# Moving constants, a residual addition and FFN work between engines in a fused linear-attention and bilinear-FFN block

## The chip, the core and the metric

The kernel runs on one core of a Trainium2 chip. Its engines work in parallel, each through its own list of instructions in order, and wait for one another by semaphores: TensorE (PE in the profile) multiplies matrices into PSUM, VectorE (DVE), ScalarE (ACT) and GpSimd (POOL) work element by element, and SyncE (SP) issues the DMA transfers. PSUM has 8 banks of 128 x 512 float32; SBUF holds everything else. The metric is the device time of one execution in microseconds (us), lower is better.

## What is computed

x is 2048 x 512; all data are float32. c and w_mod give six vectors of 512: shifts sa and sb, scales ca and cb, gates ga and gb.

```python
x = A_x
mod = (_silu(c) @ w_mod).reshape(c.shape[0], 6, 1, -1)
sa, ca, ga, sb, cb, gb = (mod[:, 0], mod[:, 1], mod[:, 2], mod[:, 3], mod[:, 4], mod[:, 5])
h = _layernorm(x, axis=-1) * (1 + ca) + sa
x = x + ga * _A_ref(h, A_wqkv, A_wo)
h = _layernorm(x, axis=-1) * (1 + cb) + sb
x = x + gb * _B_ref(h, B_w_gate, B_w_up, B_w_down)
```

`_A_ref` is linear attention with 32 heads of 16: with phi(t) = (t + 1 where t > 0, else exp(t)) + 1e-6 it forms, for each head, kv = phi(k)^T v and z = the sum of phi(k) over all tokens, then o = phi(q) kv / (phi(q) z + 1e-6), and multiplies by wo. `_B_ref` is (h w_gate) * (h w_up), times w_down, with 1376 hidden features.

## The kernel before

**Tiling.** The 2048 tokens are 4 chunks of 4 token tiles of 128. A float32 operand of a product is split into a high part (rounded to the matmul's format by a copy on ACT, L167) and a low part (the rest, a subtraction on DVE or POOL, L168), and each product is three matmuls: high by high, high by low, low by high. `bank()` gives one of four working PSUM banks and `acc_bank()` one of four accumulation banks. All large SBUF tiles share 99 slots; a tile waits until the slot that it takes is free. The order of the instructions on each engine is the order of the program text: the schedule is written out by hand.

**The token loop (L361 to L404).** v is never formed: the loop sums phi(k)^T times the normalized x over all 16 token tiles in the four accumulation banks (`t_tile`). Step i projects the keys of tile i + 2 (`proj`, 12 matmuls), in some steps also queries, prepares phi (`phi_a`: three ACT operations, Relu, Exp and the addition of 1e-6; `phi_b`: one on DVE) and multiplies tile i. In step j = 1 of a chunk the next chunk is transposed and modulated (`Norm.transpose`, `Norm.modulated`): for each of four column blocks ACT applies scale and shift (L240), DVE casts the high part (L241) and subtracts (L242). `extra` hangs other work on single steps: splits of wq and wv, and the loads and sums of the remaining modulation vectors (`mod_start`).

**Between loop and FFN (L405 to L498).** wo is loaded and split, the sums are turned into the four 512 x 128 products `wp` that carry kv, wo and ga, and `den_p`, `den_r`, `den_b`, `den_c` divide phi(q) by its denominator: a product with z (on POOL for most tiles), a sum over each head, a reciprocal, and a multiplication in place.

**Attention output (`y_step`).** For token tile i, `turn` transposes phi(q) and splits it, `y_a` multiplies it by `wp` into an accumulation bank, and `y_b` adds x to the bank on DVE (L532), writes x and takes the row statistics for the second norm.

**FFN.** The 1376 hidden features are 11 tiles of 128 (the last 96). The first eight are worked off in pairs over two chunks at once, with seven block products in place of eight (`block`, L848; the loop at L978 has 8 steps of two blocks). The last three, `lone`, are worked off chunk by chunk in `ffn` (L592): for each f the gate and up products (24 matmuls into two banks), their product on DVE, its split, and the down product of the f before. `Left` prepares sums of four column blocks for the pair stage; for the second pair of chunks its steps are in the list `trickle`, from which `some(n)` takes n at given points. At those points (`s1`, `s2`, `s3`, `down`, `s4` of a block) there are also the split of the next weights (`right_split`: four ACT copies, four POOL subtractions), their loads and their sums.

## Time and profile before

| what | us |
|---|---|
| median of 3 runs | 595.63 (595.63 to 596.22) |
| the profiled execution | 595.54 |
| its span, first to last instruction | 593.8 |
| outside the span | 1.7 |
| TensorE, first matmul | 12.0 after the start |
| DVE, ACT, POOL busy | 400.6, 283.8, 207.1 |

Busy time of an engine is the union of its instructions' bars. Matmuls are pipelined: a bar of 0.39 us can begin 0.23 us after the one before, so bars overlap. Below, "idle" for PE is the time that no bar covers, and a wait is put down to the instruction whose end released it. A chain of waits is followed back from the last instruction of the program.

### The profile page before, as it was taken

Reading aid. Unit: us, or ns where it says so; the run is one execution under the profiler, and the core shown is the slowest. Engines: PE = TensorE matmul, PEld = TensorE weight load, DVE = VectorE, ACT = ScalarE, POOL = GpSimd, SP = SyncE. Lnnn points to the kernel's source line nnn. Section 1 sums busy time; section 2 is a strip of 40 time slices with the busy share of each in tenths; the row PEclk is TensorE's granted clock in tenths of the full one; section 3 lists DMA queues with packets and bytes.
Section 4 is the critical chain, followed back from the end, with each engine's and each line's share of the span. In section 5 each row is a group of like instructions: output and inputs, shape, how many; then the busy total and the mean of one; then the engine's idle time right before and its main releaser. Section 6 shows DMA issues by size and latency. Waiting matters only on the chain.

```text
span 593.8 us, 7258 instructions
## 1 busy us (share of the span) xinstructions
PE 563.6 (95%) x2548; PEld 456.1 (77%) x2548; DVE 400.6 (67%) x621; ACT 283.8 (48%) x489; POOL 207.1 (35%) x186
## 2 busy tenths in 40 slices
PE   1999998999899998999999999999999999999997
PEld 1777886788788876887877788878778888888885
DVE  6877396964879799865757548778785454545475
ACT  3497684747562821533152445453553444444430
POOL 1323012220412380000000108676684848383710
PEclk9999999999989999999999999999999999999999
DMA  8900122220500100002603215532259736120003
GB/s 287 349 2 1 54 88 72 71 72 0 148 1 0 72 1 1 36 36 86 198 36 107 71 38 141 177 130 84 97 189 357 279 106 213 35 72 0 2 2 141
DMA packets 46501, 57.17 MB, mean 96 GB/s; under 512 B 5152, under 2 KB 23584, under 8 KB 46464
## 3 DMA queue, kind: packets, MB, share of 16 engines
q1 hardware_dynamic: 46464, 56.71, 29.2%
q8 instruction: 20, 0.33, 0.2%
q14 instruction: 17, 0.14, 0.1%
HBM read 40.96 MB, written 15.73 MB: 95 GB/s over the span
## 4 chain that ended last, share of the span: by engine, by line
PE 74%; DVE 14%; ACT 8%; issue 2%; DMA 1%; POOL 0%; SPq 0%; DVEq 0%; ACTq 0%; POOLq 0%
PE bank L816 25%; PE acc L832 5%; PE acc L834 5%; PE acc L833 5%; PE bank L180 3%; PE bank L181 3%; PE bank L182 3%; PE bank L613 3%; PE bank L614 3%; PE bank L612 3%; PE acc L182 2%; PE acc L180 2%; PE acc L181 2%; DVE w L168 2%; PE acc L295 1%
## 5 line engine op out<-in xcount | busy, mean ns | idle before, releaser
L816 PE MATMUL bank<-h,w 128*128 128x512 f32 x672 | 156.4, 390 | 3.3 <-ACT kh L167 1.3
L816 PEld LDWEIGHTS bank<-h,w 128*128 128x128 f32 x672 | 125.8, 188 | 31.2 <-ACT bank L822 2.8
L168 POOL TENSOR_TENSOR w<-raw,w 128x512 fp32r<-128x512 f32 x26 | 37.3, 1454 | 75.6 <-ACT w L167 57.6
L167 ACT ACTIVATE kh<-phi 128x512 fp32r<-128x512 f32 (+1 forms) x60 | 37.2, 628 | 55.2 <-DVE phi L621 34.3
L802 POOL TENSOR_TENSOR w<-raw,w 128x256 fp32r<-128x256 f32 (+1 forms) x28 | 30.8, 1101 | 81.2 <-ACT w L795 81.2
L588 DVE TENSOR_TENSOR x<-acc,x 128x512 f32<-128x512 f32 x80 | 50.7, 680 | 4.1 <-PE acc L834 3.5
L168 DVE TENSOR_TENSOR kl<-phi,kh 128x512 fp32r<-128x512 f32 (+1 forms) x60 | 47.1, 794 | 9.4 <-ACT kh L167 8.7
L822 ACT ACTIVATE bank<-bank 128x512 f32<-128x512 f32 x32 | 18.6, 582 | 67.5 <-PE bank L816 67.5
L834 PE MATMUL acc<-w,kl 128*128 128x512 f32 x128 | 49.9, 390 | 0.0
L832 PE MATMUL acc<-w,kh 128*128 128x512 f32 x128 | 49.8, 389 | 0.0
L833 PE MATMUL acc<-w,kh 128*128 128x512 f32 x128 | 49.8, 389 | 0.0
L180 PE MATMUL bank<-w,h 128*128 128x512 f32 x120 | 48.7, 406 | 0.0
L181 PE MATMUL bank<-w,h 128*128 128x512 f32 x120 | 47.3, 394 | 1.0 <-DVE w L168 1.0
L182 PE MATMUL bank<-w,h 128*128 128x512 f32 x120 | 47.5, 396 | 0.0
L281 POOL TENSOR_TENSOR z<-z,phi 128x512 f32<-128x512 f32 x15 | 21.3, 1421 | 72.0 <-DVE phi L267 68.0
L217 POOL TENSOR_TENSOR rstd<-ve,half 128x4 f32<-128x4 f32 x8 | 9.8, 1231 | 96.3 <-DVE ve L216 96.3
L802 POOL TENSOR_TENSOR w<-t,w 128x512 fp32r<-128x512 f32 x28 | 39.3, 1405 | 0.0
L613 PE MATMUL bank<-h,w 128*128 128x512 f32 (+1 forms) x96 | 37.7, 392 | 0.3 <-DVE h L242 0.2
L612 PE MATMUL bank<-h,w 128*128 128x512 f32 (+1 forms) x96 | 37.8, 393 | 0.0
L614 PE MATMUL bank<-h,w 128*128 128x512 f32 (+1 forms) x96 | 37.5, 391 | 0.0
L225 ACT ACTIVATE n<-x,nmr,rstd 128x512 f32<-128x512 f32 x32 | 23.7, 803 | 20.9 <-DVE nmr L220 20.9
L903 DVE TENSOR_TENSOR g<-bank,u 128x512 f32<-128x512 f32 x16 | 11.0, 687 | 33.6 <-PE bank L816 33.6
(144 smaller groups left out, 1224.7 us busy)
## 6 DMA issues: line engine op xcount, KB each, us to landing
raw<-in_w_mod_dram SPq DMA_DIRECT2D x24, 256.0 KB, 3.8
raw<-in_B_w_down_dram SPq DMA_DIRECT2D x18, 256.0 KB, 3.0
x<-in_A_x_dram SPq DMA_DIRECT2D x16, 256.0 KB, 5.4
kept<-f SPq DMA_DIRECT2D x16, 256.0 KB, 2.0
f<-kept SPq DMA_DIRECT2D x16, 256.0 KB, 3.7
raw<-in_B_w_gate_dram SPq DMA_DIRECT2D x32, 128.0 KB, 3.4
raw<-in_B_w_up_dram SPq DMA_DIRECT2D x32, 128.0 KB, 3.6
side_s<-h SPq DMA_DIRECT2D x16, 256.0 KB, 2.1
```

The costliest lines, as they stand in the source:

```text
L168: (low or nc.vector).tensor_tensor(l, src, f32(h), op=ALU.subtract)
L180: nc.tensor.matmul(ps, ah, bh, start=i == 0, stop=False)
L181: nc.tensor.matmul(ps, ah, bl, start=False, stop=False)
L182: nc.tensor.matmul(ps, al, bh, start=False, stop=i == n - 1)
L612: nc.tensor.matmul(ps[:n], w[0][:, k], hh, start=k == 0, stop=False)
L613: nc.tensor.matmul(ps[:n], w[0][:, k], hl, start=False, stop=False)
L614: nc.tensor.matmul(ps[:n], w[1][:, k], hh, start=False, stop=k == KD - 1)
L802: sub = lambda out, x, y: (on or nc.gpsimd).tensor_tensor(out, x, f32(y), op=ALU.subtract)
L816: mm = lambda x, y, **kw: nc.tensor.matmul(ps, x[:, k], y, skip_group_check=True, **kw)
L832: nc.tensor.matmul(dn[j], hh[:, a:b], dh, start=i == 0, stop=False)
L833: nc.tensor.matmul(dn[j], hh[:, a:b], dl, start=False, stop=False)
L834: nc.tensor.matmul(dn[j], hl[:, a:b], dh, start=False, stop=i == len(hs) - 1)
```

## The change

1. *Constant of phi.* The ACT addition of 1e-6 goes from `phi_a`. For k the constant enters as the bias of the copy that makes the high part, and in the low part's operation; z gets 2048 times the constant. For q it enters in `den_c`, and the denominator gets `den0`, computed once.
2. *Residual.* `y_seed` copies x into the bank ahead of the product (ACT), the matmuls accumulate on it, and `y_b` copies the sum back to x (ACT), with the statistics read from PSUM. Where the seed lies in a working bank, a matmul opens it first.
3. *Token loop.* Norms, transposes and modulation of the next chunk are spread over steps j = 3, 0 and 1; modulation vectors are loaded one to three steps ahead of their sums; wo is loaded at step 12 and split at step 14.
4. *Unpaired f tiles.* `ffn` is parted into `gate_up` and `down`. Gate and up products stand between the y tiles, q projections 11 to 15 are placed anew, and the down products of a chunk come together.
5. *Engines.* Most products of `den_p` move from POOL to DVE. `modulated` writes the high part with a second ACT operation unless `cast` names DVE.
6. *Pair stage.* The `trickle` steps come ahead of `right_split` at the `s3` points, with other counts; the second weights' first split moves to the first block; the last chunk's down products lie in the first two blocks.

```diff
+        def modulated(self, scale, shift, *ks, keep=None, cast=None):
...
                 nc.scalar.activation(f, self.ps[k], AF.Identity, scale=scale[:, k:k + 1], bias=shift[:, k:k + 1])
-                nc.vector.tensor_copy(h, f)
+                if cast:
+                    cast.tensor_copy(h, f)
+                else:
+                    nc.scalar.activation(h, self.ps[k], AF.Identity, scale=scale[:, k:k + 1], bias=shift[:, k:k + 1])
                 nc.vector.tensor_tensor(l, f, f32(h), op=ALU.subtract)
...
         nc.scalar.activation(t, ps, AF.Relu, scale=-1.0)
         nc.scalar.activation(t, t, AF.Exp, scale=-1.0)
-        nc.scalar.activation(t, t, AF.Identity, bias=eps_phi)
...
     def k_split(i):
-        kx[i] += [B("kh", dt=F32R), B("kl", dt=F32R)]
-        split(phk.pop(i), *kx[i][2:])
+        h, l = B("kh", dt=F32R), B("kl", dt=F32R)
+        phi = phk.pop(i)
+        nc.scalar.activation(h, phi, AF.Identity, bias=eps_phi)
+        nc.vector.scalar_tensor_tensor(l, phi, EPS_PHI, f32(h), op0=ALU.add, op1=ALU.subtract)
+        kx[i] += [h, l]
...
-    def mod_start(v):
...
-        mod_acc(accs[v], load_mod(v), range(KD))
...
-             6: lambda: mod_start(2), 8: lambda: rows.update({2: mod_row(2, accs[2])}),
-             7: lambda: mod_start(3), 10: lambda: cols.update({3: col_out(3, mod_col(accs[3], bank()), 0.0)}),
-             9: lambda: mod_start(4), 12: lambda: cols.update({4: col_out(4, mod_col(accs[4], bank()), 1.0)}),
-             11: lambda: mod_start(5), 13: lambda: rows.update({5: mod_row(5, accs[5])})}
+             6: lambda: mod_load(2), 8: lambda: (mod_part(2, 0, 1), mod_load(3)),
+             9: lambda: (mod_part(2, 2, 3), mod_load(4)),
+             10: lambda: (mod_part(3, 0, 1, 2), mod_load(5)),
+             11: lambda: (mod_part(3, 3), mod_part(4, 0, 1), rows.update({2: mod_row(2, accs[2])})),
+             12: lambda: (raw_o.extend(load(wo_v[k], "raw") for k in range(KD)), mod_part(4, 2, 3), cols.update({3: col_out(3, mod_col(accs[3], bank()), 0.0)})),
+             13: lambda: (mod_part(5, 0, 1, 2), cols.update({4: col_out(4, mod_col(accs[4], bank()), 1.0)})),
+             14: lambda: (mod_part(5, 3), wo_s.extend(split_raw(x) for x in raw_o)), 15: lambda: rows.update({5: mod_row(5, accs[5])})}
...
-        if more and j == 0 and i:
-            nx.nmr_of()
-            nx.xhat(0, 1, 2)
-        if more and j == 1:
-            nx.xhat(3)
+        if i + 1 < NT:
+            k_split_x(i + 1)
+            k_split(i + 1)
+        if more and j == 0:
+            nx.xhat(2, 3)
+        if more and j < 2:
             t_tile(i, 0, 1)
-            nx.transpose(0, 1, 2, 3)
-            nx.modulated(ca, sa, 0, 1, 2, 3)
-            norm.append(nx)
+            nx.transpose(2 * j, 2 * j + 1)
+            nx.modulated(ca, sa, 2 * j, 2 * j + 1, cast=nc.vector)
+            norm[ch + 1:] = [nx]
...
             nx.stats(2, 3)
             nx.rstd_of()
-        if i + 1 < NT:
-            k_split_x(i + 1)
-            k_split(i + 1)
+            nx.nmr_of()
+            nx.xhat(0, 1)
...
-            nc.scalar.activation(zb, zps, AF.Copy)
-        t_tile(i, *range(2 if more and j == 1 else 0, KD))
+            nc.scalar.activation(zb, zps, AF.Identity, bias=eps_z)
+        t_tile(i, *range(2 if more and j < 2 else 0, KD))
         if i in extra:
             extra[i]()
-    raw_o = [load(wo_v[k], "raw") for k in range(KD)]
...
+    def den_z():
+
+        nc.vector.reduce_sum(den0, zb.rearrange("p (h i) -> p h i", i=DH), axis=AX.X)
+        nc.vector.tensor_scalar(den0, den0, EPS_PHI, EPS_DEN, op0=ALU.mult, op1=ALU.add)
...
-        nc.vector.tensor_scalar(dens[ch], dens[ch], EPS_DEN, None, op0=ALU.add)
+        nc.vector.tensor_tensor(dens[ch], dens[ch], den0.unsqueeze(1).to_broadcast([P, NJ, NH]), op=ALU.add)
...
-            nc.vector.tensor_tensor(p3, p3, dens[ch][:, j].unsqueeze(2).to_broadcast([P, NH, DH]), op=ALU.mult)
+            nc.vector.scalar_tensor_tensor(p3, p3, EPS_PHI, dens[ch][:, j].unsqueeze(2).to_broadcast([P, NH, DH]),
+                                           op0=ALU.add, op1=ALU.mult)
...
+    den_z()
+    den_a(0, 0, 1, on=nc.vector)
     ps = proj(6, wq)
...
-    den_a(0, 0, 1, on=nc.vector)
     q_b(6)
     q_b(7)
+    den_a(0, 2, on=nc.vector)
     ps = proj(8, wq)
...
-    den_a(0, 2, on=nc.vector)
+    den_p(0, 3, on=nc.vector)
     split(kvf, *kvp)
-    den_a(0, 3, on=nc.vector)
-    wo_s = [split_raw(r) for r in raw_o[:2]]
-    wo_s += [split_raw(r, low=nc.gpsimd) for r in raw_o[2:]]
+    den_r(0, 3)
+    den_b(0)
     q_a(8, ps)
-    q_tile(9)
-    den_b(0)
+    ps = proj(9, wq)
     q_b(8)
     w_out(0, 1)
-    q_b(9)
+    q_a(9, ps)
     den_c(0)
     w_out(2, 3)
+    q_b(9)
     q_tile(10)
...
+    def y_seed(i, of=acc_bank):
+
+        yps[i] = of()
+        if of is bank:
+
+            nc.tensor.matmul(yps[i], wp[0][0][:, :P], wp[0][0], start=True, stop=True)
+        nc.scalar.activation(yps[i], xts[i // NJ][i % NJ], AF.Copy)
...
     def y_a(i):
-        yps[i] = acc_bank()
+        if i not in yps:
+            y_seed(i)
         pq = pqs.pop(i)
-        product(yps[i], [(cut(pq, k * P, (k + 1) * P), wp[k]) for k in range(KD)])
+        for k in range(KD):
+            (ah, al), (bh, bl) = cut(pq, k * P, (k + 1) * P), wp[k]
+            for x, y in ((ah, bh), (ah, bl), (al, bh)):
+                nc.tensor.matmul(yps[i], x, y, start=False, stop=k == KD - 1 and x is al, skip_group_check=True)
...
     def y_b(i):
         ch, j = divmod(i, NJ)
-        xt = xts[ch][j]
-        nc.vector.tensor_tensor(xt, yps.pop(i), xt, op=ALU.add)
-        norm2[ch].stats(j)
-
-    def y_step(i, *more, late=(), q=None, turn=True):
+        ps = yps.pop(i)
+        nc.scalar.activation(xts[ch][j], ps, AF.Copy)
+        norm2[ch].stats(j, of=ps)
...
         y_a(i)
+        if i + 1 in tps:
+            turn_h(i + 1)
+            turn_l(i + 1)
         if i - 1 in yps:
             y_b(i - 1)
-        if i + 1 in tps:
-            turn_h(i + 1)
         if q is not None:
             q_a(q, ps)
+        if seed and i + 1 < NT:
+            y_seed(i + 1)
         for do in more:
             do()
-        if i + 1 in tps:
-            turn_l(i + 1)
...
-    def ffn(ch, pre={}, post={}, tail=None, leave=False):
...
+    def gate_up(ch, f):
+
+        n = fts[f][1]
+        gps, ups = bank(), bank()
...
+        def rest():
...
+            hs[ch, f] = h, l
+        return rest
+
+    def down(ch, js=range(NJ), ahead={}, parts=(lone,)):
+
+        dn = {j: acc_bank() for j in js}
+        for step, (part, j) in enumerate((part, j) for part in parts for j in js):
+            for do in ahead.get(step, ()):
...
+            a, b = j * P, (j + 1) * P
+            for f in part:
+                n = fts[f][1]
+                (hh, hl), (dh, dl) = hs[ch, f], wf[f][2]
+                nc.tensor.matmul(dn[j], hh[:n, a:b], dh[:n], start=f == lone[0], stop=False)
+                nc.tensor.matmul(dn[j], hh[:n, a:b], dl[:n], start=False, stop=False)
+                nc.tensor.matmul(dn[j], hl[:n, a:b], dh[:n], start=False, stop=f == lone[-1])
+        return lambda: evac(ch, dn, js)
...
-    ps13 = proj(13, wq)
+    f0, f1, f2 = lone
+    turn_a(0)
+    ps = proj(11, wq)
+    turn_h(0)
+    turn_l(0)
+    y_seed(0)
+    den_c(1)
+    q_a(11, ps)
+    q_b(10)
+    y_step(0, lambda: den_c(2), lambda: q_b(11))
+    y_step(1, lambda: den_c(3))
+    y_step(2, lambda: split_gu(f0, nc.gpsimd))
+    y_step(3, lambda: scale_down(f0), turn=False, seed=False)
+    ps12 = proj(12, wq)
     y_b(3)
     norm2[0].rstd_of()
-    turn(4)
-    scale_down(lone[0])
+    den_a(1, 0, on=nc.vector)
+    q_a(12, ps12)
+    ps13 = proj(13, wq)
+    q_b(12)
     q_a(13, ps13)
-    ps = proj(14, wq)
+    ps14 = proj(14, wq)
     norm2[0].nmr_of()
     ln2_xhat(0)
+    split_down(f0, nc.gpsimd)
     q_b(13)
-    split_down(lone[0], nc.gpsimd)
-    y_a(4)
-    ln2_turn(0, 0, 1, 2, 3)
+    den_a(1, 1, 2, on=nc.vector)
+    ln2_turn(0, 0, 1, cast=nc.vector)
     ps15 = proj(15, wq)
-    q_a(14, ps)
+    q_a(14, ps14)
+    den_a(1, 3, on=nc.vector)
+    ln2_turn(0, 2, 3, cast=nc.vector)
+    den_b(1)
     q_b(14)
...
+    den_c(4)
     q_a(15, ps15)
-    ffn(0, {0: [lambda: q_b(15), lambda: den_c(5, 6, 7), lambda: split_down(lone[1], nc.gpsimd)],
-               1: [lambda: scale_down(lone[2]), lambda: split_ffn(lone[2]), lambda: den_a(2, 0, 1)],
-               2: [lambda: den_a(2, 2, 3), lambda: den_b(2), lambda: den_p(3, 0, 1)]},
-        {1: [lambda: turn(5)], 2: [lambda: den_r(3, 0, 1), lambda: den_p(3, 2, 3)]})
...
+    split_gu(f1, nc.gpsimd)
+    g = gate_up(0, f0)
+    q_b(15)
+    den_c(5)
+    scale_down(f1)
+    g()
+    turn(4)
+    y_seed(4)
+    split_gu(f2)
+    g = gate_up(0, f1)
+    den_a(2, 0, on=nc.vector)
+    den_c(6)
+    split_down(f1, nc.gpsimd)
+    g()
+    y_step(4, lambda: scale_down(f2), lambda: den_a(2, 1, on=nc.vector))
+    g = gate_up(0, f2)
+    split_down(f2)
+    den_c(7)
+    den_a(2, 2, on=nc.vector)
+    g()
+    y_step(5)
+    y_step(6, lambda: den_a(2, 3, on=nc.vector))
+    y_step(7, turn=False, seed=False)
+    y_b(7)
+    norm2[1].rstd_of()
+    den_b(2)
+    take = down(0)
+    ln2_nx(1)
+    den_c(8, 9, 10)
+    turn(8)
+    y_seed(8, bank)
+    take()
+    ln2_turn(1, 0, 1)
+    y_step(8)
+    ln2_turn(1, 2, 3)
+    y_step(9)
+    g = gate_up(1, f0)
+    den_a(3, 0, 1, on=nc.vector)
+    den_c(11)
+    g()
+    g = gate_up(1, f1)
+    den_a(3, 2, on=nc.vector)
+    g()
+    y_step(10)
+    g = gate_up(1, f2)
+    den_a(3, 3, on=nc.vector)
+    g()
+    y_step(11, turn=False, seed=False)
     y_b(11)
     norm2[2].rstd_of()
-    ffn(1, {0: [lambda: den_c(13)], 1: [lambda: ln2_nx(2), lambda: den_c(14, 15)]},
-        {1: [lambda: ln2_turn(2, 0, 1)], 2: [lambda: turn(13), lambda: norm2[2].transpose(2, 3)]},
-        lambda: norm2[2].modulated(cb, sb, 2, 3, keep=kept[2]))
...
+    den_b(3)
+    take = down(1)
+    ln2_nx(2)
+    den_c(12, 13, 14)
+    turn(12)
+    y_seed(12, bank)
+    take()
+    ln2_turn(2, 0, 1)
+    y_step(12, lambda: den_c(15))
+    ln2_turn(2, 2, 3)
+    y_step(13)
+    g = gate_up(2, f0)
+    g()
+    y_step(14)
+    g = gate_up(2, f1)
+    g()
+    y_step(15)
     y_b(15)
     norm2[3].rstd_of()
...
-    ffn(2, {0: [lambda: first[0].sum("s1", "s3", "s2", "s4")],
-            1: [lambda: ln2_nx(3), lambda: first[0].split("s3", "s4")],
-            2: [lambda: first[1].sum("s1", "s3", "s2", "s4")]},
-        {0: [lambda: first[0].split("s1", "s2")], 1: [lambda: ln2_turn(3, 0, 1)],
-         2: [lambda: norm2[3].transpose(2, 3), lambda: right_sums(0, nc.vector)]},
-        lambda: norm2[3].modulated(cb, sb, 2, 3, keep=kept[3]))
+    g = gate_up(2, f2)
+    right_sums(0, nc.vector)
+    ln2_nx(3)
+    first[0].sum("s1", "s3", "s2", "s4")
+    g()
+    right_split(0, nc.vector)
+    take = down(2, ahead={2: [lambda: ln2_turn(3, 0, 1)], 5: [lambda: ln2_turn(3, 2, 3)]}, parts=((f0, f1), (f2,)))
+    first[0].split("s1", "s2", "s3", "s4")
+    take()
...
-    rest = ffn(3, {0: [lambda: first[1].split("s1", "s2")],
-                   1: [lambda: first[1].split("s3", "s4"), lambda: right_sums(1, nc.vector)],
-                   2: [lambda: trickle.extend(left(0))]},
-               {0: [lambda: right_split(0, nc.vector)], 2: [lambda: right_split(1, nc.vector), lambda: some(2)]}, leave=True)
+    g = gate_up(3, f0)
+    first[1].sum("s1", "s3", "s2", "s4")
+    g()
+    g = gate_up(3, f1)
+    first[1].split("s1", "s2", "s3", "s4")
+    g()
+    trickle.extend(left(0))
+    g = gate_up(3, f2)
+    right_sums(1, nc.vector)
+    g()
+    rest = [lambda js=js: down(3, js) for js in ((0, 1), (2, 3))]
...
         if n == 0:
             at["s3"].pop(0)
+            at["s1"] = [lambda: right_split(1, nc.vector)]
             at["s4"].append(lambda: some(2))
         else:
-            at["s3"].append(lambda: some((4, 4, 5)[n - 1] if n < 4 else 0))
+            at["s3"].insert(0, lambda: some((4, 5, 5)[n - 1] if n < 4 else 0))
         if n and steps[n - 1][0] != cs:
             at["s1"] = [lambda: fetch(stash, side, "a22", "s4")]
         g = block(side, rights[2 * n], down=down_of(0), at=at)
-        at = {"s3": [lambda: right_split(2 * n + 2), lambda: right_load(2 * n + 3),
-                     lambda: ahead.update(ds=split_pair(draw)), lambda: some((0, 2, 3)[n] if n < 3 else 0)],
+        at = {"s3": [lambda: some((0, 3, 3)[n] if n < 3 else 0), lambda: right_split(2 * n + 2), lambda: right_load(2 * n + 3),
+                     lambda: ahead.update(ds=split_pair(draw))],
               "s4": [lambda: right_sums(2 * n + 3)]}
         if n == 0:
-            at["s1"] = [at["s3"].pop(0)]
+            at["s1"] = [at["s3"].pop(1)]
...
```

102 lines of the change are left out of this document (27 added, 75 removed).

## The prediction

> **What bounds the kernel now.** I read the head of the page first, then the busy time of each engine by stage, then the list of who waits for whom on TensorE.
>
> ```profile
> span 593.8 us, 7258 instructions
> PE 563.6 (95%) x2548; PEld 456.1 (77%) x2548; DVE 400.6 (67%) x621; ACT 283.8 (48%) x489; POOL 207.1 (35%) x186
> PE 74%; DVE 14%; ACT 8%; issue 2%; DMA 1%; POOL 0%; SPq 0%; DVEq 0%; ACTq 0%; POOLq 0%
> ```
>
> TensorE is busy for 95% of the span, yet 22% of the chain lies on DVE and ACT. The matmul work is nearly the same after the change, so the question is which idle stretches of PE go and which come. I cut the span where the kernel changes its kind of work: start, start of the token loop, rest of the loop, kv and output weights, first attention outputs, first FFN chunk, middle chunks, end of the single f tiles, paired f tiles with side work, the same without, tail.
>
> ```profile
> core 0: us, PE busy (x) PEld busy (x) DVE busy (x) ACT busy (x) POOL busy (x), PEclk, DMA share, GB/s
> 0.00:26.00 26.00, 12.63 (x52) 10.65 (x52) 18.22 (x37) 10.02 (x15) 6.03 (x15) 1.00 0.93 330
> 26.00:61.00 35.00, 33.21 (x149) 26.32 (x149) 26.63 (x49) 28.97 (x48) 10.77 (x8) 1.00 0.07 25
> 61.00:140.00 79.00, 76.67 (x348) 60.70 (x347) 52.04 (x81) 50.30 (x82) 15.26 (x11) 1.00 0.21 67
> 140.00:172.00 32.00, 29.67 (x148) 24.55 (x147) 26.92 (x38) 20.90 (x37) 8.46 (x6) 0.95 0.25 69
> 172.00:205.00 33.00, 32.99 (x161) 26.86 (x160) 24.49 (x46) 20.38 (x33) 7.48 (x6) 1.00 0.09 33
> 205.00:240.00 35.00, 32.34 (x149) 24.83 (x148) 32.46 (x46) 7.72 (x14) 14.64 (x9) 1.00 0.00 1
> 240.00:316.00 76.00, 76.00 (x369) 61.86 (x368) 50.29 (x93) 28.90 (x45) 3.62 (x3) 1.00 0.23 77
> 316.00:342.00 26.00, 25.67 (x116) 19.97 (x115) 16.10 (x30) 9.88 (x19) 2.87 (x4) 1.00 0.34 102
> 342.00:460.00 118.00, 114.72 (x501) 93.47 (x500) 84.44 (x104) 56.44 (x106) 69.35 (x60) 1.00 0.47 152
> 460.00:576.00 116.00, 116.00 (x513) 96.11 (x512) 59.44 (x89) 49.00 (x92) 68.21 (x65) 1.00 0.29 91
> ```
>
> Length minus PE busy gives PE's idle time: 1.79, 2.33, 2.33, 0.01, 2.66, 0, 0.33, 3.28 and 0 us from the second row on; 12.73 us in all. The 13.4 us of the first row lie ahead of the changed work, and what follows 576 us is not touched.
>
> ```profile
> PE bank L180 <- DVE h L267: 2.0, 1, 2.0
> PE bank L232 <- ACT n L225: 1.5, 2, 0.8
> PE acc L602 <- ACT kh L167: 1.5, 1, 1.5
> PE acc L293 <- ACT kh L167: 1.4, 1, 1.4
> PE bank L181 <- DVE w L168: 1.3, 3, 0.7
> PE bank L816 <- ACT kh L167: 1.3, 1, 1.3
> PE bank L816 <- DVE g L903: 1.2, 1, 1.2
> PE acc L150 <- DVE f L145: 12.0, 1, 12.0
> 561.03 9.52 PE bank L816 x42
> 163.74 0.59 PE L182 MATMUL bank<-w,xl 128*128 128x512 f32 x1
> 167.12 0.44 PE L181 MATMUL bank<-w,h 128*128 128x512 f32 x1
> ```
>
> The waits are few and short, always for ACT or DVE, never for a load after the first 12 us. The row of 42 matmuls gives the pace: 9.52/42 = 0.227 us. A matmul's own bar is 0.39 us, so each wait costs 0.16 us more than its gap; the whole list has 16 after the first 12 us, 2.6 us. Behind the 2.0 us wait of L180 eight matmuls start 0.42 us apart (163.74 to 167.12), which loses 8 x 0.2 = 1.6 us. What can be won is thus about 12.7 + 2.6 + 1.6 = 16.9 us. By the Trainium skill, "TensorE: Matmul & The Clock Gate", "Why this matters for your kernels", the clock falls only after idle gaps above about 3 us. By that the 1.6 us would not have been lost; the rows show that 2.0 us was enough here, and waits of 1.4 and 1.5 us left no such trace.
>
> **The change, stage by stage.** The durations:
>
> ```profile
> L264 ACT ACTIVATE phi<-phi,eps_phi 128x512 f32<-128x512 f32 x16 | 11.6, 724 | 0.5
> L167 ACT ACTIVATE kh<-phi 128x512 fp32r<-128x512 f32 x56 | 34.6, 627 | 42.7 <-DVE phi L621 21.7 <-DVE phi L856 16.3 <-DVE phi L267 4.6
> L263 ACT ACTIVATE h<-h 128x512 f32<-128x512 f32 x16 | 10.1, 633 | 0.5
> L822 ACT ACTIVATE bank<-bank 128x512 f32<-128x512 f32 x32 | 18.6, 582 | 67.5 <-PE bank L816 67.5
> L217 POOL TENSOR_TENSOR rstd<-ve,half 128x4 f32<-128x4 f32 x8 | 9.8, 1231 | 96.3 <-DVE ve L216 96.3
> L240 ACT ACTIVATE f<-bank,col,col 128x512 f32<-128x512 f32 x32 | 22.8, 776 | 12.4 <-PE bank L232 9.9 <-DVE col L155 2.5
> L532 DVE TENSOR_TENSOR x<-acc,x 128x512 f32<-128x512 f32 x16 | 10.9, 681 | 4.7 <-PE acc L182 4.6
> L416 POOL TENSOR_TENSOR f<-h,zb 128x512 f32<-128x512 f32 x12 | 18.5, 1577 | 0.0
> L416 DVE TENSOR_TENSOR f<-h,zb 128x512 f32<-128x512 f32 x4 | 2.7, 684 | 0.0
> 92.90 3.23 DVE L145 SCALAR_TENSOR_TENSOR f<-raw,sc,f 128x512 f32<-128x512 f32 x3
> 193.38 2.92 ACT L225 ACTIVATE n<-x,nmr,rstd 128x512 f32<-128x512 f32 x4
> ```
>
> *Token loop (26 to 140).* The 32 constant additions of L264 go: 0.72 us of ACT each, 23 us in all. In the 16 k tiles the constant moves into the high part's copy, which gets a bias (0.63 to 0.72), net -0.62 us a tile; in the 16 q tiles it moves into DVE's den_c at no extra instruction. The fused three-operand forms that DVE gets I take at 0.68 to 1.08 (a third of the 3.23 row) against 0.68, so 0 to 0.4 us each and near 0, off PE's path. The four modulated columns of a chunk now go two by two over two steps, and the row norms start one step earlier. That takes both waits for n L225 (0.7 and 0.8) and the 1.4 us wait for kh L167: that kh stood behind three norms which stood behind DVE's multiplies of the modulation weights (92.90, 3.23 us), now one to three steps after their load. The 16 loads of w_mod and the 4 of wo keep their order on SP; wo, issued last, comes before its use by two steps of about 5.9 us (24 matmuls and 8 transposes), so I put no cost on them. The new wait: DVE's nmr stands right behind POOL's pow (1.23 us) with phi of the next k tile behind it; PE has 12 to 24 matmuls (2.7 to 5.4 us) in front, so 0. In the first stage the wait for w L168 is for DVE's splits of wq, which lose nothing; what ACT wins there reaches PE only in part. I take **1.0** of 1.79 for the first stage (0 to 1.8) and **3.0** for the second: 2.3 of idle, the rest bars that overlap (2 to 4).
>
> *Kv and output weights (140 to 172).* The wait of 2.0 us ended at q's phi_b (L267), which stood on DVE behind two wo splits and the den chain. The wo splits move to step 14 of the loop, the den products ahead of the kv chain. DVE then has 3.6 us (five operations of 0.68 and a short one) before the four scaled kv columns; working the queue through, the last low part is ready about 0.4 us after PE wants it. 2.3 + 1.6 - 0.4 = **3.5** won (2.5 to 4).
>
> *First attention outputs (172 to 205).* The residual goes to ACT: per token tile a copy x to PSUM and one back (0.58, L822, which writes PSUM, to 0.63, L167) replace DVE's 0.68 (L532). Statistics now read PSUM: L532 with a PSUM operand takes as long as L416 without (681 and 684 ns), so I take no more for it; up to 0.3 us would still lie beside PE. A tile's PE work is 12 matmuls and 4 transposes, 3.2 us; ACT's three copies are 1.8 us, DVE's split, statistics and den_c 2.1 us: both fit. But before the first FFN norm ACT must now take q 12 and q 13 ahead of the four norms (2.92 us for four): q 13's product ends 5.4 us after the last y product, plus 1.2 of Relu and Exp (L263), plus 2.9, is 9.5, while PE has three products, 8.2 us. New wait 1.3, and 0.35 for banks held by the transposed columns: **-1.7** (-3.3 with a slowed clock, to 0).
>
> By the Trainium skill, "PSUM — Partial Sum Buffer", "Terms", no two engines may read one bank at once, and y_b now has ACT's copy and DVE's statistics on the same bank. No row here shows two such reads. By that rule the statistics start 0.6 us later in each tile, an estimate, and the term stays as it is because ACT is last; the rule returns under the rivals.
>
> *First FFN chunk (205 to 240).* DVE is busy 32.46 of 35 us, the highest share of any stage. Two things make it so: the y additions and den work, and POOL, beside which operations of the same form take up to 1.77 us:
>
> ```profile
> 212.79 1.77 DVE L569 TENSOR_TENSOR raw<-raw,row 96x512 f32<-96x512 f32 x1
> 437.54 1.77 DVE L168 TENSOR_TENSOR h<-s,h 128x512 fp32r<-128x512 f32 x1 [1.69 <-ACT h L167]
> 438.97 0.62 ACT L167 ACTIVATE h<-s 128x512 fp32r<-128x512 f32 x1
> ```
>
> The 12 den products leave POOL (12 x 1.58 = 18.9 us) for DVE (12 x 0.68 = 8.2), spread over three chunks; the y additions leave DVE. From the first gate to the last y tile of the chunk PE has 72 + 48 matmuls and 16 transposes, 29 us; DVE 32 wide operations of 0.68 and some 3 us more beside POOL, 25. The down products wait until all three f tiles are ready, and y tiles lie between, so PE has something else at each of the three waits here. 2.66 + 3 x 0.16 = **3.1** won (1 to 3.1).
>
> *Middle chunks (240 to 316).* Nothing is idle. Casts leave DVE, a second ACT operation per column (0.78, L240) comes. After y 7 (and 11) PE has down, 36 matmuls or 8.2 us, over the statistics and norms; then one turn of y 8, waiting for a bank behind DVE, and again one before y 9: about 0.5 us per chunk, **-1.0** (-3 to 0). The two dummy matmuls that open a seed in a working bank: 2 x 0.227 = **-0.45**.
>
> *End of the single f tiles (316 to 342).* After y 15 PE has 32 us (132 matmuls, 16 transposes), DVE some 37 wide operations of 0.68 and eight of half the width, 28; **+0.3** (-2 to +0.3).
>
> *Paired tiles (342 to 460).* The side splits go ahead of the weight splits on ACT. Before, they were last: ACT's five copies ended at 439.6, DVE's subtractions ran beside POOL's at 1.2 to 1.8 us each, and the product that frees the bank (g L903) came 1.2 us late. First in line, they run before POOL starts, at 0.6. The weight splits start up to 5 x 0.52 = 2.6 us later, and POOL's low parts have 4 us or more until read. **+3.4** of 3.28 + 4 x 0.16 (1 to 3.9).
>
> Sum: 1.0 + 3.0 + 3.5 - 1.7 + 3.1 - 1.0 - 0.45 + 0.3 + 3.4 = 11.15 us. The profiled execution took 595.5 us (1.7 outside the span); 595.5 - 11.1 = 584.4. The median of the runs is 0.1 above it: **584.5**.
>
> **Rivals.**
> *All of it lands* and the new waits hide: the 16.9 us go, less 0.45: 579. For: PE's queue is long everywhere. Against: the first-chunk count above. Waits under 0.16 us, which no busy row shows, could add 3: 576. Chance 0.14.
>
> *ACT takes DVE's place* between 172 and 342: the 3.1 is not won, the first turn costs 3.3, the middle 2.0. 11.1 - 3.1 - 1.6 - 1.0 = 5.4, so 590. For: ACT gains about 3 operations per tile there. Against: ACT is busy 7.72 of 35 us. With the bank rule exposed at all four turns, 4 x 0.6 = 2.4 more, it is 592.5. Chance 0.17.
>
> *Slower:* in each of three chunks the four columns need 8 ACT operations, 8 x 0.776 = 6.2 us, in order behind copies and seeds. If only one y product (2.7) lies beside them, PE waits 3.5 us and then runs slow for 1.6: 3 x 5.1 = 15.3 against 12.1 otherwise won, 598.5. It turns the sign at 4 us per chunk. Against: two y products and down lie there. Chance 0.10.
>
> *It does not do what it says:* the waits end at other things than those named, and nothing moves, 595.5 within 1. Chance 0.04.
>
> **How the numbers follow.** My forecast (580 to 589) has 0.55. The range 576 to 592 leaves out the slower case, the unchanged one and a part of the ACT case, under 0.2. A measurement of this kernel tells about 0.2% (1.2 us) from no change. Faster 0.55 + 0.14 + 0.17 = 0.86, within 0.04, slower 0.10.
>
> **What would show it.** No wait of bank L180 for q's phi at the wo stage and no half-speed steps behind it; no waits for n or kh in the loop after 61 us; DVE's share in the first FFN chunk below 0.85; no PE wait for g or the bank copy between 380 and 450; one new wait of about 1.3 us of a transpose for ACT's n ahead of the first FFN chunk. Wrong it would be if PE waits for ACT's modulated columns at each chunk, or a load appears on the chain.

## The result: 582.67 us, 2.2% faster

The median of four runs went from 595.66 us to **582.67** (582.31 to 583.39); the ratio is 0.9781, with a 95% interval of 0.9764 to 0.9798. The forecast was 584.5, in a range of 576 to 592. The profiled execution took 582.31 us, its span 580.4; before, the span was 593.8.

The head of the page and the chain of waits of the changed kernel:

```profile
span 580.4 us, 7236 instructions
PE 560.0 (96%) x2550; PEld 457.3 (79%) x2550; DVE 384.8 (66%) x609; ACT 287.1 (49%) x501; POOL 182.7 (31%) x173
PE 87%; DVE 7%; ACT 3%; issue 1%; DMA 1%; POOL 0%; SPq 0%; DVEq 0%; POOLq 0%
```

TensorE does the same work, but 87% of the chain lies on it now, where it was 74%. The busy time by stage, cut where the changed kernel passes from one kind of work to the next (columns: stretch, length, then busy time and instructions of PE, PEld, DVE, ACT and POOL, the granted clock, DMA share, GB/s):

```profile
26.00:61.00 35.00, 34.16 (x154) 26.84 (x153) 27.06 (x48) 25.10 (x42) 10.39 (x8) 1.00 0.08 28
61.00:134.00 73.00, 72.21 (x339) 59.57 (x338) 57.35 (x87) 42.34 (x69) 15.96 (x11) 1.00 0.23 72
134.00:164.00 30.00, 29.95 (x154) 24.61 (x152) 23.83 (x39) 16.61 (x30) 0.00 (x0) 1.00 0.27 73
164.00:191.00 27.00, 25.94 (x124) 20.82 (x124) 17.45 (x32) 16.20 (x28) 5.22 (x4) 1.00 0.06 21
191.00:229.00 38.00, 37.57 (x171) 29.71 (x171) 30.09 (x52) 17.98 (x32) 5.38 (x4) 1.00 0.04 15
229.00:297.00 68.00, 67.39 (x327) 54.91 (x326) 37.14 (x66) 32.21 (x54) 1.01 (x1) 1.00 0.24 78
297.00:328.00 31.00, 31.00 (x146) 24.50 (x145) 24.91 (x46) 18.35 (x31) 1.03 (x1) 1.00 0.31 96
328.00:446.00 118.00, 118.00 (x522) 97.74 (x521) 77.83 (x105) 57.77 (x109) 70.09 (x63) 1.00 0.47 148
```

Length minus PE busy is 0.84, 0.79, 0.05, 1.06, 0.43, 0.61, 0 and 0 us: 3.8 in all, where 12.7 stood before. The granted clock is 1.00 in every one of these rows; the stage of kv and output weights had 0.95. The list of who waits for whom on TensorE has shrunk with it (its larger rows behind the first 12 us; columns: us in total, times, longest):

```profile
PE bank L234 <- ACT n L227: 1.5, 4, 0.4
PE bank L182 <- DVE h L244: 0.7, 1, 0.7
PE bank L529 <- DVE xl L537: 0.6, 2, 0.3
PE bank L634 <- ACT f L242: 0.4, 1, 0.4
```

To compare stage by stage I need a measure that holds bars which overlap and matmuls at half clock as well. For each matmul of the trace I take the time to the start of the next one, less the pace of the uninterrupted stretch (0.227 us for 512 columns, 0.11 for a transpose of 128), and call the sum over a stage its **stall**. Stages are matched by their work as nearly as the new order allows: between 201 and 342 us gate products, y tiles and down products change places, so those three rows hold 153, 271 and 222 matmuls before and 177, 318 and 145 after, and only their sum (2.7 won, 2.4 forecast) compares like with like.

| stage (before; after) | stall before | stall after | won | forecast |
|---|---|---|---|---|
| loop start (26:61; 26:58) | 3.09 | 2.31 | 0.8 | 1.0 |
| rest of loop (61:139.1; 58:134.2) | 5.65 | 1.91 | 3.7 | 3.0 |
| kv, output weights (139.1:175.3; 134.2:164.7) | 5.13 | 1.68 | 3.4 | 3.5 |
| first attention outputs (175.3:201.1; 164.7:191) | 0.90 | 2.30 | -1.4 | -1.7 |
| first FFN chunk (201.1:238; 191:230) | 3.96 | 0.95 | 3.0 | 3.1 |
| middle chunks (238:293; 230:297) | 0.50 | 1.67 | -1.2 | -1.0 |
| end of the single f tiles (293:342.6; 297:328.4) | 1.13 | 0.28 | 0.85 | 0.3 |
| paired tiles (342.6:460; 328.4:446) | 4.53 | -0.09 | 4.6 | 3.4 |
| two matmuls that open seeds | | | -0.45 | -0.45 |

The column adds up to 13.3 us, against 13.4 by the spans; its last row is taken at 0.227 us a matmul, not measured apart. The terms came out near the forecast; whether they came for the forecast's reasons is what the experiments ask. Times below are medians of 4 to 12 runs; each ratio is to the kernel before on the same chip.

### The profile page after: what moved, and what is told of

The parts are those of the page before. It is cut to its first block, busy times and chain, and to the rows that moved or that the text cites. A ratio compares the mean times of both kernels' runs of the same rounds, so it can differ in the third digit from the quotient of the medians.

```text
span 580.4 us, 7236 instructions
## 1 busy us (share of the span) xinstructions
PE 560.0 (96%) x2550; PEld 457.3 (79%) x2550; DVE 384.8 (66%) x609; ACT 287.1 (49%) x501; POOL 182.7 (31%) x173
## 4 chain that ended last, share of the span: by engine, by line
PE 87%; DVE 7%; ACT 3%; issue 1%; DMA 1%; POOL 0%; SPq 0%; DVEq 0%; POOLq 0%
PE bank L891 26%; PE acc L559 7%; PE acc L909 5%; PE acc L907 5%; PE acc L908 5%; PE bank L634 4%; PE bank L635 4%; PE bank L636 4%; PE bank L183 4%; PE bank L184 4%; PE bank L182 4%; PE acc L658 2%; PE acc L659 2%; PE acc L660 2%; PE acc L302 2%; PE acc L300 2%
## 5 line engine op out<-in xcount | busy, mean ns | idle before, releaser
L170 POOL TENSOR_TENSOR w<-raw,w 128x512 fp32r<-128x512 f32 x24 | 33.5, 1416 | 89.6 <-DVE mv L212 47.7
L877 POOL TENSOR_TENSOR w<-raw,w 128x256 fp32r<-128x256 f32 (+1 forms) x28 | 33.0, 1177 | 73.5 <-ACT w L870 61.0
L169 ACT ACTIVATE kh<-phi 128x512 fp32r<-128x512 f32 (+1 forms) x44 | 27.1, 628 | 48.6 <-DVE phi L643 35.0
L170 DVE TENSOR_TENSOR kl<-phi,kh 128x512 fp32r<-128x512 f32 (+1 forms) x44 | 33.3, 770 | 9.5 <-ACT kh L169 8.7
```

What stands on the lines that cost most here:

```text
L170: (low or nc.vector).tensor_tensor(l, src, f32(h), op=ALU.subtract)
L877: sub = lambda out, x, y: (on or nc.gpsimd).tensor_tensor(out, x, f32(y), op=ALU.subtract)
```

## Experiments: one part undone at a time

**The order in the paired stage.** Undone, all else as changed:

```diff
-            at["s3"].insert(0, lambda: some((4, 5, 5)[n - 1] if n < 4 else 0))
+            at["s3"].append(lambda: some((4, 5, 5)[n - 1] if n < 4 else 0))
```

(and the same in the second block of each step.)

> The changed kernel with only the order of the trickle put back: in the paired stage the left sides' splits stand behind the right side's split again, with the same counts. Theory (the forecast's term for the paired stage, 3.4 us there, measured as 4.6 us of stall gone between 342 and 460 us): the order alone carries it, so the time goes from 582.7 us to 585.5 to 587.5, and the waits of matmuls for a late split come back in the paired stage alone. Rival: the stall went because the work ahead of the stage ended earlier or because one split moved between pairs (counts 4, 4, 5 and 2, 3 to 4, 5, 5 and 3, 3); then 582.5 to 583.5.

Measured: 590.88 us, ratio 0.9914 (0.9902 to 0.9927): **8.2 us** slower than the changed kernel, more than either theory gave. The profiled execution took 589.41 us, 7.1 more than that of the changed kernel, and all of that lies in the paired stage, whose stall is 7.0 us; what puts the median higher than this execution is not shown. The list of waits of that kernel between 328 and 456 us:

```profile
PE bank L891 <- ACT kh L169: 3.7, 2, 2.5
PE bank L891 <- DVE g L978: 2.3, 2, 1.2
```

The longest, 2.5 us, has no equal in the kernel before. Its timeline on DVE, POOL and PE (start, length in us, engine, line, operation):

```profile
384.64 1.77 DVE L170 TENSOR_TENSOR h<-f,h 128x512 fp32r<-128x512 f32 x1
386.34 1.76 DVE L170 TENSOR_TENSOR h<-s,h 128x512 fp32r<-128x512 f32 x1
388.02 0.68 DVE L931 TENSOR_TENSOR phi<-bank,g 128x512 f32<-128x512 f32 x1
385.83 3.40 POOL L170 TENSOR_TENSOR w<-raw,w 128x512 fp32r<-128x512 f32 x2
389.44 5.71 PE L891 MATMUL bank<-h,w 128*128 128x512 f32 x24 [2.47 <-ACT kh L169]
```

Last in line, the left sides' subtractions run on DVE while POOL makes the low parts of the weights, at 1.77 us in place of 0.69, and the product of the block (L931) stands behind them. The changed counts put three of them at this point where the kernel before had two, so the old order costs more with the new counts: 7.0 us against 4.5. The row of L931 shows something else: it runs beside POOL too, at 0.68. It reads one operand from PSUM and one from SBUF, the slow ones read two from SBUF. By the Trainium skill, "SBUF — State Buffer", "SBUF: two separate sides", VectorE and GpSimd share a pair of ports that the first comer holds for its whole instruction, and VectorE needs the pair, among other cases, beside a GpSimd operation that reads SBUF when both its inputs lie in SBUF. These rows agree as to which operations are slowed: 1.77 us with two inputs in SBUF, 0.68 with one.

**The order alone, in the kernel before**, with the counts of before:

```diff
-            at["s3"].append(lambda: some((4, 4, 5)[n - 1] if n < 4 else 0))
+            at["s3"].insert(0, lambda: some((4, 4, 5)[n - 1] if n < 4 else 0))
```

> The kernel before with only the order of the trickle changed: in the paired stage the left sides' splits stand ahead of the right side's split, with the counts of before. Theory (order alone carries the paired stage's 4.6 us): 591 to 592.6 us against 595.7, and the stalls between 342 and 460 us gone. Rival (the order needs the other parts of the change, since what it moves forward then delays the weight split in turn): 594.7 to 596.

Measured: 591.01 us, ratio 0.9929 (0.9917 to 0.9942), 4.6 us faster than before, and the stall between 342 and 460 us went from 4.53 to -0.07. The order alone carries the whole term, and needs nothing else of the change.

**den_p of chunks 1 to 3 back on POOL.**

```diff
-            (on or nc.gpsimd).tensor_tensor(pzs[ch, j], phq[ch * NJ + j], zb, op=ALU.mult)
+            (on if ch == 0 else nc.gpsimd).tensor_tensor(pzs[ch, j], phq[ch * NJ + j], zb, op=ALU.mult)
```

> The changed kernel with den_p of chunks 1 to 3 (12 products of 128x768) back on GpSimd. Theory (the first FFN chunk's 3.0 us came back because VectorE got its own shared path free: its products beside GpSimd's took longer): the stalls of 191 to 230 us rise by 1 to 3 us, VectorE's mean durations there rise, the time is 583.7 to 585.7. Rival (the order of the chunk's work, y tiles between the gate products, is what freed it; which engine does den_p is not felt): 582.2 to 583.2.

(The products are 128x512, as the rows below show.) Measured: 589.51 us, ratio 0.9896 (0.9882 to 0.9909), **6.8 us** slower, above both theories. But nothing of it comes from chunks 2 and 3: all lies between 180 and 203 us. The timeline there:

```profile
186.91 1.29 POOL L170 TENSOR_TENSOR w<-raw,w 128x512 fp32r<-128x512 f32 x1 [5.95 <-ACT w L169]
188.16 3.75 POOL L437 TENSOR_TENSOR f<-h,zb 128x512 f32<-128x512 f32 x3
189.48 0.69 DVE L443 TENSOR_REDUCE den<-f 128x32 f32<-128x512 f32 x1 [5.27 <-POOL f L437]
191.32 0.87 DVE L244 CAST h<-f 128x512 fp32r<-128x512 f32 x1
195.43 1.64 DVE L247 TENSOR_TENSOR h<-f,h 128x512 fp32r<-128x512 f32 x1
```

POOL waits 5.95 us for ACT's high part of the down weights (ACT has the four norms in front), and the products of den stand behind that split. DVE's reduction takes the product, waits 5.27 us for it, and the casts of the first FFN operands stand behind the reduction: the first comes at 191.32, where the changed kernel has it at 187.87. That is a wait handed through two queues. Behind it come subtractions at 1.64 in place of 0.69 beside POOL, and a slower clock (the busy time between 192 and 202 us, 0.83 in the third column from the end):

```profile
192.00:202.00 10.00, 6.85 (x16) 3.80 (x17) 9.83 (x14) 2.54 (x5) 4.68 (x3) 0.83 0.14 51
```

To see whether the place in the queue matters, the same four products of chunk 1 went to POOL with the last three **ahead** of the weight split:

```diff
-    den_a(1, 0, on=nc.vector)
+    den_a(1, 0)
...
+    den_p(1, 1, 2, 3)
     split_down(f0, nc.gpsimd)
     q_b(13)
-    den_a(1, 1, 2, on=nc.vector)
+    den_r(1, 1, 2)
...
-    den_a(1, 3, on=nc.vector)
+    den_r(1, 3)
```

> The changed kernel with den_p of chunk 1 alone on GpSimd (4 products), and its last three ahead of the split of the first down weights in GpSimd's queue, where in the kernel of u_pool they stood behind it. Theory A (the 6.8 us of u_pool are a wait in a queue: VectorE's reduction stood ahead of the first FFN casts and waited 5.3 us for a product behind a weight split): 582.5 to 584. Theory B (they are contention of VectorE with GpSimd's products, 1.5 and 1.6 us for operations of 0.4 and 0.7): 585.5 to 589.5.

Measured: 582.15 us (581.89 to 582.68), ratio 0.9764 (0.9745 to 0.9784): nothing is lost. POOL does the four products in one go, and the first cast waits for its own operand from ACT and no longer for a reduction:

```profile
179.94 5.05 POOL L437 TENSOR_TENSOR f<-h,zb 128x512 f32<-128x512 f32 x4
184.40 1.27 DVE L443 TENSOR_REDUCE den<-f 128x32 f32<-128x512 f32 x2
188.02 0.94 DVE L244 CAST h<-f 128x512 fp32r<-128x512 f32 x1 [2.35 <-ACT f L242]
```

So which engine makes these products is worth nothing in the changed kernel; where they stand in the queue is worth 6.8 us. The earlier place takes away the wait and also the company of POOL's products for the casts, so the two are not parted; of the 6.8 us the one wait for POOL is 5.27.

**The same move alone, in the kernel before.**

```diff
-            (on or nc.gpsimd).tensor_tensor(pzs[ch, j], phq[ch * NJ + j], zb, op=ALU.mult)
+            (on or nc.vector).tensor_tensor(pzs[ch, j], phq[ch * NJ + j], zb, op=ALU.mult)
```

> The kernel before with one thing changed: den_p of chunks 1 to 3 runs on VectorE (12 more products of about 0.68 us there) and no longer on GpSimd. Theory (VectorE's operations of 0.68 us took up to 1.77 us beside GpSimd's products, so VectorE gains more than it takes on): the stall of the first FFN chunk, 3.96 us, falls by 1 to 2.5, the time is 593 to 594.8. Rival (VectorE was simply full, and 12 more operations make it fuller; contention is worth less than they cost): 595.7 to 598, with longer waits for kh in that chunk.

Measured: 597.25 us (12 runs), ratio 1.0015 (1.0002 to 1.0029): no faster, slower if anything. The waits of that kernel between 172 and 240 us:

```profile
PE acc L182 <- DVE xl L517: 2.2, 1, 2.2
PE bank L509 <- DVE h L439: 1.9, 1, 1.9
PE acc L602 <- ACT kh L167: 0.9, 1, 0.9
```

The wait for kh of a single f tile does fall, from 1.5 to 0.9, but the turn at the chunk's end rises from 0.9 to 1.9, and the stall of the first FFN chunk stays where it was, 3.99 against 3.96. The loss stands ahead of it: a y tile waits 2.2 us for its low part behind two products of den, DVE is busy for 9.76 of the 10 us from 180 on, the granted clock there is 0.83, and the stall of the first attention outputs rises from 0.9 to 4.9. More than half of that is won back earlier, in the stretch of kv and output weights, where the stall falls from 5.1 to 2.4. There POOL's four products ran beside the short operation that begins `den_b` (L431), and q's phi stood behind it; without them the operation is short, and the wait for phi is 0.94 us in place of 2.0 (two rows of the kernel before, then two of this one):

```profile
159.79 5.43 POOL L416 TENSOR_TENSOR f<-h,zb 128x512 f32<-128x512 f32 x4
160.30 1.29 DVE L431 TENSOR_SCALAR den<-den 128x128 f32<-128x128 f32 x1
160.38 0.21 DVE L431 TENSOR_SCALAR den<-den 128x128 f32<-128x128 f32 x1
162.18 0.50 PE L180 MATMUL bank<-w,xh 128*128 128x512 f32 x1 [0.94 <-DVE h L267]
```

So relief from POOL's company is real, but it comes in another stage than the theory said, and twelve more operations on DVE cost at least what it brings.

**The residual back on DVE** (no seed, no matmul that opens one, statistics from SBUF):

```diff
-        nc.scalar.activation(xts[ch][j], ps, AF.Copy)
-        norm2[ch].stats(j, of=ps)
+        xt = xts[ch][j]
+        nc.vector.tensor_tensor(xt, ps, xt, op=ALU.add)
+        norm2[ch].stats(j)
```

> The changed kernel with the attention residual back as an addition on VectorE (no seed by ScalarE in PSUM, no seed matmul, the norm's statistics from SBUF). Theory (VectorE has 0.79 of the first FFN chunk and room for it; what the seed saves on VectorE it costs in two 0.23 us matmuls and in the statistics' wait for ScalarE's copy, 4.9 us over 14): 582.0 to 583.2. Rival (the 14 additions of about 0.8 us taken off VectorE are what removed the first FFN chunk's stalls): 584.2 to 586, with matmul waits for VectorE back between 191 and 230 us.

Measured: 582.77 us (582.58 to 583.0), ratio 0.9786 (0.9773 to 0.9799): the same as with the residual in PSUM. The two seed matmuls saved are given back in turns that wait longer (for DVE h L460 1.1 us in place of 0.3). What the residual's move costs DVE can be read in the changed kernel's groups:

```profile
L211 DVE BATCH_NORM_STATS2 st<-acc 128x6 f32<-128x512 f32 x14 | 9.7, 693 | 4.9 <-ACT x L564 4.9
```

The statistics wait for ACT's copy of the same bank, 4.9 us over 14 tiles. By the Trainium skill, "PSUM — Partial Sum Buffer", "Terms", two engines must not read one bank at once. What the row shows is that a semaphore keeps the two apart, 0.35 us a tile where the forecast's estimate was 0.6; what would happen without it no run here shows. The wait lies beside PE's work and cost nothing.

**The constant of phi back in its own operation.**

```diff
         nc.scalar.activation(t, t, AF.Exp, scale=-1.0)
+        nc.scalar.activation(t, t, AF.Identity, bias=eps_phi)
```

(with the plain split and the plain `den_b` and `den_c` that belong to it.)

> The changed kernel with the constant of phi added in its own ScalarE operation again (one more of about 0.6 us per q or k half projection) and no folding into the splits and den. Theory (the operation sat in the chain from projection to split, so its return is felt where ScalarE's order ends a wait: at the token loop's start and in the steps without cover, and in the first attention outputs): 583.7 to 585.7, with matmul waits for kh or for the norm n back in the loop. Rival (moving the q projections beside the loop gave all the cover that was needed; the operation itself lies beside other work everywhere): 582.2 to 583.2.

Measured: 586.99 us, ratio 0.986 (0.984 to 0.9879): **4.3 us** slower, above the theory's range. It is spread over the loop's start (stall 2.31 to 3.50), the rest of the loop (1.91 to 2.88), kv and output weights (1.68 to 2.36), and the first attention outputs (2.30 to 3.22), 3.8 us together. A further 0.5 us is one wait for a load at 456 us, which the kernel with POOL's products ahead of the split shows too (0.46), so it isn't phi's. The waits of that kernel between 26 and 136 us:

```profile
PE bank L234 <- ACT n L227: 2.2, 3, 1.4
PE bank L182 <- DVE h L244: 1.2, 1, 1.2
```

ACT is busy for 55 to 72% of the first four of these stages in the changed kernel, yet operations put into its queue ahead of a norm come out as longer waits of the transposes.

**The output weights loaded and split behind the loop, as before.**

```diff
+    raw_o.extend(load(wo_v[k], "raw") for k in range(KD))
...
+    wo_s.extend(split_raw(x) for x in raw_o[:2])
+    wo_s.extend(split_raw(x, low=nc.gpsimd) for x in raw_o[2:])
```

> The changed kernel with the output weights loaded and split after the token loop, as before. Theory (in before, the stretch with kv and the output weights lost 5.1 us, of which one idle gap of about 2 us and the half-speed matmuls behind it; the early load is what removed them): 584.7 to 587 us, with a gap of 1 us or more between 134 and 170 us and a granted clock below 0.95 there. Rival (the gap was ScalarE's and VectorE's phi work of the q projections that now runs in the loop; with those gone the splits find room anyway): 582.4 to 583.4.

Measured: 583.96 us, ratio 0.9808 (0.9794 to 0.9821): 1.3 us slower, less than the theory's least and more than the rival's most. The wait for phi is back, but short, and the granted clock stayed at 1.00:

```profile
PE bank L182 <- DVE h L271: 1.0, 1, 1.0
```

**Early weights and the loop's order alone, in the kernel before.** The norm of the next chunk a step earlier and its columns turned two by two (as in the change), the split of k ahead of it, wo loaded at step 12 and split at 14; the modulation sums stay in one piece (`mod_start`), and phi stays as before.

```diff
-        if more and j == 0 and i:
-            nx.nmr_of()
-            nx.xhat(0, 1, 2)
...
+        if more and j < 2:
+            t_tile(i, 0, 1)
+            nx.transpose(2 * j, 2 * j + 1)
+            nx.modulated(ca, sa, 2 * j, 2 * j + 1)
...
+             14: lambda: wo_s.extend(split_raw(x) for x in raw_o)}
```

> The kernel before with two parts of the change alone: the order of the next chunk's norm in the token loop (normalised a step earlier, two columns turned in each of two steps, k's split ahead of it), and the output weights loaded at step 12 and split at step 14. ScalarE's phi operation, the spread of the mod work and all behind 172 us stay as before. Theory (order and cover carry these stages: 3.7 us between 61 and 140, of which putting phi's operation back returned only 0.5, and 3.4 between 140 and 172, of which the late weights returned 1.3): the loop behind 61 us falls from 5.65 to 2 to 3.2 us of stall, the weights' stretch from 5.1 to 2 to 3.8, the time is 589.8 to 592. Rival (these stalls need the shorter phi chain or the spread mod work to go): 593.5 to 595.7, with matmuls still waiting for kh and n.

Measured: 595.67 us, ratio 0.9997 (0.9983 to 1.0012): no change, as the rival had it, but made of two opposite halves. In the stretch of kv and output weights the stall fell from 5.13 to 1.5, the whole term, with one wait left. In the loop behind 61 us it **rose**, from 5.65 to 7.36. The waits on either side (first row: 61 to 142 us, second: 142 to 174 us):

```profile
PE bank L232 <- ACT n L225: 4.3, 3, 3.7
PE bank L180 <- DVE h L267: 0.6, 1, 0.6
```

And the timeline of the long one:

```profile
84.56 1.20 DVE L143 TENSOR_SCALAR f<-raw,sc 128x512 f32<-128x512 f32 x1
85.79 2.33 DVE L145 SCALAR_TENSOR_TENSOR f<-raw,sc,f 128x512 f32<-128x512 f32 x3
92.34 0.16 DVE L220 SCALAR_TENSOR_TENSOR nmr<-mv,rstd 128x4 f32<-128x4 f32 x1 [1.20 <-POOL rstd L217]
98.10 0.33 PE L232 MATMUL bank<-ident,n 128*128 128x128 f32 x1 [3.66 <-ACT n L225]
```

A whole modulation vector, 3.5 us of DVE, stands ahead of the statistics, and the norm that is now wanted a step earlier comes 3.7 us late. In the changed kernel, where the modulation sums are cut up and moved, nmr stands at 87.31 in the same step. That the earlier norm pays only together with these sums is read from the two traces; no run moves the sums alone.

## Two versions beyond the change

**The norm's statistics one step earlier still.** In the changed kernel two transposes wait at 92 us for n. Its timeline, DVE and POOL:

```profile
86.26 1.02 POOL L219 TENSOR_TENSOR rstd<-ve,half 128x4 f32<-128x4 f32 x1 [3.12 <-DVE ve L218]
87.31 0.16 DVE L222 SCALAR_TENSOR_TENSOR nmr<-mv,rstd 128x4 f32<-128x4 f32 x1 [1.20 <-POOL rstd L219]
```

```diff
-            nx2.stats(0, 1)
+            nx2.stats(0, 1, 2, 3)
+            nx2.rstd_of()
...
-            nx.stats(2, 3)
-            nx.rstd_of()
```

> The changed kernel with the statistics and the power of the next chunk's first norm taken one step earlier in the token loop (VectorE's statistics of tiles 2 and 3 and GpSimd's power in step j=2 rather than j=3). Theory (at 91.6 to 93.6 us two transposes waited about 0.6 us each for the norm n, whose chain hung on GpSimd's power with no q projection beside it): that wait goes, 581.3 to 582.0 us. Rival (the same work only moves a wait of the step before, or the transposes are next held by something else): 582.4 to 583.2.

Measured: **581.33** us (581.01 to 581.9), ratio 0.9765 (0.9752 to 0.9778). The list of waits has none between 61 and 134 us. POOL's power now runs a step ahead:

```profile
82.92 1.02 POOL L219 TENSOR_TENSOR rstd<-ve,half 128x4 f32<-128x4 f32 x1 [5.30 <-DVE ve L218]
```

**Cover for the first FFN chunk.** With that, y tile 4 goes between the q projections and the first FFN products:

```diff
+    turn(4)
+    y_seed(4)
+    ln2_xhat(0)
+    ps14 = proj(14, wq)
+    y_a(4)
```

(and den of chunk 1 between y tiles 0 to 3, tile 5's turn ahead of the third gate.)

> The kernel of e_norms, and in the first attention outputs y tile 4 and den of chunk 1 set between the first y tiles and the first FFN chunk, so that TensorE has a tile of its own to do while ScalarE makes the first n tiles. Theory (the new wait of 185 to 192 us, about 1.2 us for n and 0.6 us for the first f operands, is a want of cover): 579.3 to 580.7 us. Rival (the moved den products of chunk 1 make VectorE late for the first FFN turn, and the wait only changes its name): 581.3 to 582.8.

Measured: 581.22 us (580.46 to 582.36), ratio 0.9761 (0.9746 to 0.9775): hardly different, between the theory and the rival. The stall ahead of the first FFN chunk fell from 2.3 to 0.5 us, and that of the chunk itself rose from 0.9 to 2.1: tile 6 now waited for its seed. The last version puts this seed ahead of the third gate's copy:

```diff
     g = gate_up(0, f2)
+    y_seed(6)
     split_down(f2)
...
-    y_step(5)
+    y_step(5, seed=False)
```

> The kernel of e_best with the seed of y tile 6 put on ScalarE ahead of the third gate's copy. Theory (in e_best the wait of 1.5 us before the first FFN chunk went, and 0.98 us came back at 213.7 us, where y tile 6 waited for its seed behind the split of a gate): that goes too, 580.1 to 580.8. Rival (the tile then waits for its own transposed columns instead): 580.9 to 581.5.

Measured: **580.93** us (580.86 to 582.11), ratio 0.9749 (0.9728 to 0.9769). The wait went from 0.82 to 0.34 us and is now for the tile's own columns, so the rival was right for that rest:

```profile
213.63 0.73 PE L558 MATMUL acc<-w,xh 128*128 128x512 f32 x2 [0.34 <-ACT xh L532]
```

Against the changed kernel's 582.67 this is 1.7 us, 0.3%, with runs that don't overlap; against the version with the earlier statistics alone the ranges do.

## Why the prediction was right, and where it wasn't

**Paired tiles.** The mechanism was right: the order alone gives 4.6 us in the kernel before and takes more away in the changed one. The term was too small, 3.4 of 4.6. It was added up from bars that overlap and waits on the list; the gaps between starts, which count what is lost in restarting the matmuls too, were 0.2 + 0.95 + 0.2 + 1.4 + 1.3, and some of less than 0.2.

**Kv and output weights.** The size was right: 3.5 forecast, 3.4 won, and the early weights, with the loop's new order, won 3.6 in the kernel before. The cause was seen in part. The forecast put the late phi down to DVE's queue, two splits of wo and the den chain. That chain was also drawn out by POOL, 1.29 us for an operation of 0.21, and taking the den products off POOL won 2.7 in this stretch without the early weights. In the changed kernel no den product runs on POOL, which fits that undoing the early weights costs only 1.3 there: 1.0 us of wait comes back, and no slow steps behind it.

**Token loop.** Won 3.7 of 3.0 forecast, 0.8 of 1.0 at its start. Its reasons held together, not singly. The order of the norms without the rest loses 1.7 us; the modulation sums, which the forecast had as the cause of the late kh, are by the traces what makes the order pay. The sentence that put the wait for nmr behind POOL's power at 0 was wrong: at 92 us two transposes wait, 1.2 us between starts, because step 7 has no q projection to lie in front, and the statistics one step earlier took just that away. The constant of phi, for which the forecast had no term of its own, costs 4.3 us when it is put back, 3.8 of them in four stages.

**First attention outputs.** -1.7 forecast, -1.4 measured, and the new wait stands where it was put. The timeline of PE:

```profile
185.99 0.33 PE L234 MATMUL bank<-ident,n 128*128 128x128 f32 x1 [0.37 <-ACT n L227]
186.69 0.76 PE L234 MATMUL bank<-ident,n 128*128 128x128 f32 x5 [0.38 <-ACT n L227]
191.51 0.50 PE L634 MATMUL bank<-h,w 128*128 128x512 f32 x1 [0.43 <-ACT f L242]
```

Each loses 0.6 us from start to start, 1.8 in all. A y tile as cover took 1.8 away, which shows that it was a want of cover; as 1.2 came back in the next chunk, little of it was won as time.

**First FFN chunk.** The size was right, 3.0 of 3.1, and **the step that failed is its reason**: "The 12 den products leave POOL (12 x 1.58 = 18.9 us) for DVE (12 x 0.68 = 8.2), spread over three chunks; the y additions leave DVE." Neither is what was wanted. The additions back on DVE changed the time by 0.1 us, less than can be told; the products of chunks 2 and 3 back on POOL cost nothing, those of chunk 1 nothing if they stand well in the queue; and the move alone, in the kernel before, left this chunk's stall at 3.99 us. DVE's share did come down to 30.09 of 38 us, as forecast, without being the cause. As far as these two reasons go, that the size came out is luck. What remains is the other half of that paragraph, that down products wait until all three f tiles are ready and y tiles lie between. In the changed kernel no down product is on the list of waits, and before one waited 1.5 us; but this half was reached by elimination and not tried by itself, nor was the new place of the last q projections beside it. The parts undone elsewhere (phi, the early weights, the paired order) left this chunk's stall at 0.8 to 1.0 us.

**Middle chunks and seeds.** -1.2 against -1.0 forecast; the seeds' -0.45 is their number times the pace in both. The two waits for DVE xl L537 (0.6 us in the list, 0.47 each from start to start) are the turn of y 9 and y 13 that waits for the bank of the one before.

**The rivals.** ACT did not take DVE's place: no matmul waits for a modulated column at the later chunks. The slower case needed 3.5 us of wait per chunk, and the list shows 0.3. (Its sum gives 598.7, not the 598.5 on record.)

**Where the time came out below the forecast.** The sum of the stages is 2.15 us above the forecast's 11.15: 1.2 in the paired tiles, 0.7 in the loop, 0.55 at the end of the single f tiles and 0.3 in the first attention outputs, less 0.6 in the other rows.

## What to carry to other kernels

Ask of a moved operation what stands behind it in its queue, before asking how long it takes: the same four products cost 6.8 us behind a weight split and nothing ahead of it, while ahead of it either engine would do. An earlier start can be lost if what stands in front of it on some engine is not moved too, as with the norm behind a whole modulation vector. And a term that comes out at its forecast size isn't yet a reason confirmed: undo the part alone, and do it alone.
